# More weight-gradient jobs before the gradient's first stage, seven DMA transposes for its turn, and the prefix's stores on SyncE's queue

## The chip, the cores and the metric

The kernel runs on one core of one Trainium2 chip. The metric is the device time of one execution in microseconds (us), taken as the median over runs; lower is better. Times inside the kernel come from one profiled execution and count from the start of its span.

Names used throughout: PE is TensorE (matmuls), PEld its weight loads, DVE is VectorE, ACT is ScalarE, POOL is GpSimd and SP is SyncE. SP does no arithmetic; it issues DMAs, in the order of its queue. POOL issues DMAs too. A DMA moves data between the device memory and the on-chip memory, and one kind of it, the DMA transpose, turns blocks on the way.

## The reference

The kernel computes a forward pass of four sublayers (A, B, A, B) and its whole gradient.

```python
def _A_ref(q, k, v, shift_k, ssm_k, ssm_D):
    # k_shift: causal convolution of k with 4 taps per feature
    kv = k_shift * v
    # y: causal convolution of kv with ssm_k over 2048 positions, by FFT of length 4096
    y = y + kv * ssm_D[None, None, :]
    return q * y

def _B_ref(x, w1, w2):
    return silu(x @ w1) @ w2

x = A_q
x = x + _A_ref(_layernorm(x), A_k, A_v, A_shift_k, A_ssm_k, A_ssm_D)
x = x + _B_ref(_layernorm(x), B_w1, B_w2)
x = x + _A_ref(_layernorm(x), A_k, A_v, A_shift_k, A_ssm_k, A_ssm_D)
x = x + _B_ref(_layernorm(x), B_w1, B_w2)
```

The inputs are in bf16: 2048 positions by 448 features, `w1` 448 x 1792, `w2` 1792 x 448. Outputs are `x` and the gradients with respect to `A_q`, `A_k`, `A_v`, `shift_k`, `ssm_k`, `ssm_D`, `w1` and `w2` for a given `grad_out`. The convolution result `y` depends on neither `x` nor the layer, so it is computed once; its gradient is summed over both A layers and goes back through the transform once.

## The kernel before

The program has three parts.

**The prefix** (`_ssm_prefix`, about the first 95 us) computes `y`. The long convolution is a transform in two stages. Stage 1 is a matmul with `M1sb` for each of 16 values of `n2`. Its result is turned in seven groups of 16 blocks of 128 x 128 (`turn` on PE, or a DMA transpose from SP, L369). Stage 2 is a matmul with `Gsb` over 14 chunks of 1024 columns. It does this for the kernel `ssm_k` (tiles `A1K`, `Z`) and for `kv` (tiles `A1kv`, then `A1K`'s memory). For `kv`, `conv` makes the four-tap convolution on PE, copies it to `ks` on ACT (L385), stores it in the device memory as `KS_d` (L387, on POOL's queue) and multiplies it by `v` on DVE; `ks` has four buffers. The spectrum product needs the spectrum `Ka` and the same with its upper and lower 64 rows exchanged (`KB`): `_swap_halves_dma` (L249, L250) makes `KB` with two DMAs per piece, seven pieces, on POOL's queue. Both spectra are stored for the gradient (`SPEC_d`, L413 and L448, on POOL's queue). `cons_prod` copies a chunk of the `kv` spectrum, multiplies it on DVE into `pa` (with `Ka`, L451) and `pb` (with `KB`, L452), and the inverse stage 2 (L232, L233) follows on PE. After the prefix, in the top-level function, SP loads `w1sb` (two DMAs, L186 and L187) and `w2sb` (L189); they reuse the memory of `M1sb` and `v_n`.

**The main part** (`Main.run`, to about 515 us) handles the 2048 positions in four chunks `c` of four tiles `tl` of 128. It runs forward through the layers, then back. Matmuls with `w1`, `w2` and their transposes fill PE. The backward chunk of the first layer pair (`L == 0`) is `ga` (L537, with `w2T`), then `gn` (L736, with `w1T`): per tile 14 matmuls into `ps_n`, a copy on ACT (L738), and on DVE and ACT the backward of two layer norms (`ln_bwd`, L711 to L723, L751 to L754), whose result goes into `gYb`, the gradient of `y`.

**The suffix** (`_ssm_suffix`) takes `gYb` back through the transform and, woven in between, computes the gradients of `w1` and `w2`. These are 2 x 14 x 32 = 896 matmuls of 128 x 448, called *jobs* (`_job`, L900). Sixteen jobs share one loaded tile `dstat` of 512 KB. For `w2`, each of 14 feature tiles takes two: a DMA transpose of `AP_d` (L896) and a plain load of `A_d` (L898); its result is copied by ACT (L913) and stored (L914). `w1` takes `GP_d` and `GH_d` likewise (L960, L936, L928, L929). There are three `dstat` buffers in the pool `dp` and two more in `dp2`, which opens with the suffix.

Jobs are handed out by a generator. `fill(n)` puts `n` of them behind the last matmul in the main part: in `ga` for `c >= 1`, two behind the first group and one behind each of the others (8 in all), and in `gn` two behind each of four tiles. Only the jobs of the first two feature tiles (64) are open to `fill`; 56 are taken. In the suffix `weave(n)` puts `n` behind the last pinned matmul, and `_in_turn` pins PE's order. A load is traced when its first job is handed out; where buffers are free a planner may place it earlier on SP's queue, and instructions on every queue are ordered by that planner, except where `issue_after(i)` places an instruction behind `i` on `i`'s engine.

The suffix starts with 16 first-stage groups (`_fft_stage1`, L210): two matmuls into a PSUM buffer, of which there are two, and a copy to `A1g` (L111 on ACT for the first 12). Four jobs follow each. Then `A1g` is turned into `Zg` in seven groups. Groups 4, 5 and 6 are DMA transposes on SP (L1008); groups 0 to 3 are 16 transposes each on PE (L1014) and a copy; 16 jobs follow each group. `spectrum(cp)` then needs group `cp` of `Zg`, and loads two pieces of the stored spectra (`kk_c`, L1022 and L1023); `spectrum(0)` and `spectrum(1)` come first, then 16 jobs, then `inverse` and `spectrum` in alternation with jobs in between. At the end `grad_k(g)` computes eight pieces of the gradient of `A_k` on DVE (L1117, L1119) and stores them (L1123) on SP's queue, behind which the last job loads stand.

Of the kernel before, what the change touches and what calls it, by code (L numbers as in the profile page):

```python
# [11 lines left out]
BF16 = mybir.dt.bfloat16  # L12
# [5 lines left out]
P = 128  # L18
S = 2048
D = 448  # L20
F = 1792
J = 16
NT = 16
# [96 lines left out]
@with_exitstack  # L120
def kernel(
    ctx: ExitStack,
    tc: tile.TileContext,
    A_q: bass.AP,
    A_k: bass.AP,
    A_v: bass.AP,
    A_shift_k: bass.AP,
    A_ssm_k: bass.AP,
    A_ssm_D: bass.AP,
    B_x: bass.AP,  # L130
    B_w1: bass.AP,
    B_w2: bass.AP,
    grad_out: bass.AP,
    out_0: bass.AP,
    out_1: bass.AP,
    out_2: bass.AP,
    out_3: bass.AP,
    out_4: bass.AP,
    out_5: bass.AP,
    out_6: bass.AP,  # L140
    out_7: bass.AP,
    out_8: bass.AP,
):
    nc = tc.nc
    k = K()
    k.tc, k.nc = tc, nc
    k.bal = _Bal(nc)
    for nm, v in (("A_q", A_q), ("A_k", A_k), ("A_v", A_v), ("A_shift_k", A_shift_k), ("A_ssm_k", A_ssm_k),
                  ("A_ssm_D", A_ssm_D), ("B_w1", B_w1), ("B_w2", B_w2), ("grad_out", grad_out)):
        setattr(k, nm, v)  # L150
    k.outs = [out_0, out_1, out_2, out_3, out_4, out_5, out_6, out_7, out_8]
    C = make_fft_consts()

    dram = ctx.enter_context(tc.tile_pool(name="dram", bufs=1, space=DRAM))
    k.KS_d = dram.tile([S, D], BF16, name="KS_d")
    k.SPEC_d = {nm: dram.tile([128, SPEC], BF16, name=f"spec_{nm}") for nm in ("K", "KV")}
    k.N_d = [dram.tile([S, D], BF16, name=f"N_d{i}") for i in range(4)]
    k.DT_d = dram.tile([4, 2, P, NF // 2, 512], BF16, name="DT_d")
    k.A_d = dram.tile([P, NF, NT, P], BF16, name="A_d")
    k.AP_d = dram.tile([NF, P, S], BF16, name="AP_d")  # L160
    k.GH_d = dram.tile([P, NF, NT, P], BF16, name="GH_d")
    k.GP_d = dram.tile([NF, P, S], BF16, name="GP_d")

    bf = mybir.dt.np(BF16)
    m1b = np.ascontiguousarray(C["M1"], dtype=np.float32).astype(bf)
    minv = (np.transpose(m1b.astype(np.float32), (3, 1, 2, 0)) * np.float32(C["inv_scale"])).astype(bf)
    k.m1_h = nc.inline_tensor(np.ascontiguousarray(m1b.reshape(P, -1)), name="c_m1")
    gs_h = nc.inline_tensor(np.ascontiguousarray(C["Gs"].reshape(P, -1)).astype(np.float32).astype(bf), name="c_gs")
    k.minv_h = nc.inline_tensor(np.ascontiguousarray(minv.reshape(P, -1)), name="c_minv")

    keep = ctx.enter_context(tc.tile_pool(name="keep", bufs=1))
    k.ident = keep.tile([P, P], BF16, name="ident")
    make_identity(nc, k.ident[:])
    k.gs_h = gs_h
    k.rstd = [keep.tile([P, J], FP32, name=f"rstd{i}") for i in range(4)]
    k.warm = keep.tile([P, 4], FP32, name="warm")
    k.mhalf = keep.tile([P, 4], FP32, name="mhalf")
    nc.gpsimd.memset(k.mhalf[:], -0.5)
    nc.scalar.activation(k.warm[:], k.mhalf[:], ACT.Silu)
    k.wk = ctx.enter_context(tc.tile_pool(name="wk", bufs=1))  # L180
    k.dp = ctx.enter_context(tc.tile_pool(name="dp", bufs=1))
    k.yk = ctx.enter_context(tc.tile_pool(name="yk", bufs=1, side="right", reuse_waits="tile"))
    k.Ysb = k.yk.tile([P, J, D], BF16, name="Ysb", tag="Y")
    _ssm_prefix(k)
    k.w1sb = k.wk.tile([P, ND, F], BF16, name="w1sb", tag="WA")
    nc.sync.dma_start(out=k.w1sb[:, 0:3, :], in_=k.B_w1[0:384].rearrange("(c p) f -> p c f", p=P))  # L186
    nc.sync.dma_start(out=k.w1sb[:, 3, :], in_=k.B_w1[320:448])  # L187
    k.w2sb = k.wk.tile([P, NF, D], BF16, name="w2sb", tag="WB")
    nc.sync.dma_start(out=k.w2sb[:], in_=k.B_w2.rearrange("(c p) d -> p c d", p=P))  # L189
    k.psum = ctx.enter_context(tc.tile_pool(name="psum", bufs=1, space=PSUM, reuse_waits="tile"))  # L190
    k.xg = ctx.enter_context(tc.tile_pool(name="xg", bufs=1, side="right", reuse_waits="tile"))
    k.Xp = k.xg.tile([P, NT, 512], BF16, name="X", tag="X")
    k.X = k.Xp[:, :, :D]
    k.gYb = k.xg.tile([P, NT, D], BF16, name="gYb", tag="GY")
    k.bal.reset()
    with ExitStack() as es:
        m = Main(k, es)
        m.run()
    _ssm_suffix(k)
# [87 lines left out]
def _ssm_prefix(k):  # L287
# [4 lines left out]
    with ExitStack() as es:  # L292
# [81 lines left out]
        def conv(h, jq):  # L374
            ds = slice(h * DH, (h + 1) * DH)
            pc = psum.tile([P, 4, 256], FP32, name="ps_cv", tag="A", bufs=4)
            for u in range(4):
                j = 4 * jq + u
                for e in range(2):
                    for t in range(4):  # L380
                        js = (j - t) % J
                        src = kT[:, js // 4, 2 * h + e, js % 4, 1:129] if j >= t else kT[:, js // 4, 2 * h + e, js % 4, 0:128]
                        nc.tensor.matmul(pc[:, u, e * DC:(e + 1) * DC], lhsT=src, rhs=diag[:, 2 * h + e, t, :], start=(t == 0), stop=(t == 3))  # L383
            ks = work.tile([P, 4, DH], BF16, name="ks", tag="pa", bufs=4)
            nc.scalar.copy(ks[:], pc[:, :, :DH])  # L385
            bal.add("act", 0.95)
            nc.gpsimd.dma_start(out=_pm(k.KS_d[:])[:, 4 * jq:4 * jq + 4, ds], in_=ks[:])  # L387
            kvt = work.tile([P, 4, DH], BF16, name="kvt", tag="pb", bufs=4)
            nc.vector.tensor_tensor(out=kvt[:], in0=ks[:], in1=vn[:, 4 * jq:4 * jq + 4, ds], op=ALU.mult)
            bal.add("dve", 0.62)  # L390
            return kvt
# [14 lines left out]
        def cons_ka(ci, ps):  # L406
            sl = slice(ci * 1024, (ci + 1) * 1024)
            _copy(nc, bal.pick(1024), Ka[:, sl], ps[:])
            if ci % 2 == 1:
                lo, hi = (ci - 1) * 1024, (ci + 1) * 1024  # L410
                if ci > 8:
                    _swap_halves_dma(k, KB, Ka, lo, hi, nc.gpsimd)
                nc.gpsimd.dma_start(out=k.SPEC_d["K"][:, lo:hi], in_=Ka[:, lo:hi])  # L413

        k.na0 = k.dp.tile([P, 4, D], BF16, name="na0", tag="dstat", bufs=3)
        prev = None
# [10 lines left out]
                if h == 1:  # L427
                    _fft_stage2(k, Z, psum, cons_ka, range(2 * i, 2 * i + 2))
        for i in range(4):
            _swap_halves_dma(k, KB, Ka, 2048 * i, 2048 * (i + 1), nc.gpsimd)  # L430
        stage1_kv(*prev)
        A1f = A1kv[:].rearrange("p a c n s -> p a (c n s)")
        for i in range(3):
            _fft_stage2(k, Z, psum, cons_ka, range(8 + 2 * i, 10 + 2 * i))
            turn(A1f, Zkv, i)
        B1 = A1kv[:].rearrange("p a c n s -> p a (c n s)")
        Zf = A1K[:].rearrange("p a c n s -> p (a c n s)")

# [4 lines left out]
        def cons_prod(ci, ps):  # L443
# [1 line left out]
            xs = Zf[:, sl]  # L445
            _copy(nc, bal.pick(1024), xs, ps[:])
            if ci % 2 == 1:
                nc.gpsimd.dma_start(out=k.SPEC_d["KV"][:, (ci - 1) * 1024:(ci + 1) * 1024], in_=Zf[:, (ci - 1) * 1024:(ci + 1) * 1024])  # L448
            pa = work.tile([P, 1024], BF16, name="pa", tag="pa", bufs=4)
            pb = work.tile([P, 1024], BF16, name="pb", tag="pb", bufs=4)  # L450
            nc.vector.tensor_tensor(out=pa[:], in0=xs, in1=Ka[:, sl], op=ALU.mult)  # L451
# [28 lines left out]
class Main:  # L480
# [245 lines left out]
    def gn(self, c, L, ghT, nb, gres, na, hook=None):  # L726
# [5 lines left out]
        for tl in range(4):  # L732
# [6 lines left out]
            k.bal.add("act", 0.75)  # L739
            k.pe_engine = mm.ins.engine  # L740
            if L == 0:
                self.fill(2)
            if hook:
                hook(tl, mm.ins, last_u.ins)
            g1 = G[:, tl, :]
# [36 lines left out]
    def run(self):  # L782
# [29 lines left out]
        for c in range(4):  # L812
# [26 lines left out]
            na, nb = na1, nb1  # L839
            if c < 3:  # L840
                gb = gb_next
        k.jobs = _gw2(k, k.dp, range(2), [(k.dp, "dstat", 3)], first=k.go_jobs.ins)
        bb = nc.cur_bb.bb

        def fill(n):
# [119 lines left out]
def _ssm_suffix(k):  # L965
# [7 lines left out]
    with ExitStack() as es:  # L973
# [5 lines left out]

        def jobs():  # L980
            yield from k.jobs
            yield from _gw2(k, k.dp, range(2, NF), both)
            yield from _gw1(k, dp2, both)

        jobs = jobs()
# [9 lines left out]
        Z = sp.tile([P, NDH, P], BF16, name="Zg")  # L995
        ksf = k.yk.tile([P, J, D], BF16, name="ksf", tag="Y")
        B1k = A1[:].rearrange("p a c n s -> p (a c n s)").rearrange("p (q d) -> p q d", d=D)
        for n2 in range(16):
            with _in_turn(k):
                _fft_stage1(k, n2, k.gYb[:, n2, :], A1, psum, nc.scalar if n2 < 12 else None)  # L1000
            weave(4)
        with tc.tile_pool(name="sspec2", bufs=1, reuse_waits="tile") as p1:
            Zf = Z[:].rearrange("p a b -> p (a b)")
            A1f = A1[:].rearrange("p a c n s -> p a (c n s)")
            for g in (4, 0, 1, 2, 3, 5, 6):
                if g > 3:
                    with tc.issue_after(k.job_load):
                        nc.sync.dma_start_transpose(out=Z[:, 16 * g:16 * g + 16, :], in_=A1f[:, 16 * g:16 * g + 16, :].rearrange("p a b -> p (a b)"))  # L1008
                    weave(NT)
                    continue  # L1010
                pt = psum.tile([P, 16, P], BF16, name="ps_tr", **mm)
                with _in_turn(k):
                    for i in range(16):
                        nc.tensor.transpose(pt[:, i, :], A1f[:, 16 * g + i, :], k.ident[:])  # L1014
                weave(NT)
                _copy(nc, bal.pick(2048, dve_ns=0.53), Z[:, 16 * g:16 * g + 16, :], pt[:])

            def spectrum(cp):
                lo, hi = cp * 2048, (cp + 1) * 2048
# [88 lines left out]
        def grad_k(g):  # L1108
# [3 lines left out]
            for j in range(4):  # L1112
# [7 lines left out]
                    last = acc  # L1120
                else:
                    last = pj
            nc.sync.dma_start(out=out2_pm[:, 2 * g:2 * g + 2, :], in_=gk[:])  # L1123

        out3_pm = _pm(k.outs[3][0])
        out2_pm = _pm(k.outs[2][0])
# [89 lines left out]
```

## Time and profile before

| what | us |
|---|---|
| median of 4 runs | 750.69 |
| lowest and highest run | 749.1 and 752.15 |
| the profiled execution | 746.83 |
| its span, first to last instruction | 745.0 |
| PE busy, of the span | 690.6 (93%) |
| DVE busy | 507.1 (68%) |
| ACT busy | 424.3 (57%) |
| POOL busy | 61.6 (8%) |

The page gives each engine's busy time over the span. A busy engine need not be the one that sets the end: the page's chain of waits follows the last instruction back, at each step to what released it. By engine that chain is PE 46%, DVE 24%, DMA 9%, ACT 8%, time without a visible wait 7%, POOL 2%. The page's DMA table counts 172.77 MB, 149.46 MB of them on SP's and ACT's kind of queue and 22.19 MB on POOL's.

A line of a timeline reads: start, duration, engine, source line, operation, output<-input, shapes, count, and in brackets how long the engine was idle before and what released it. "SPq" is SP's instruction stream: a DMA's duration there is the time that SP spent issuing it, not the time to landing. Medians from issue to landing in this profile: 13.1 us for `KB<-Z`, 5.4 for `KS_d<-ks`, 4.8 for `Zg<-A1g`, 4.7 for `dstat<-A_d`, 5.3 for `dstat<-AP_d`.

### The profile page before, as it was taken

How to read it: one execution, taken by the hardware profiler on the slowest of the kernel's cores; microseconds unless marked ns; L12 is line 12 of the kernel's file. 1: busy time of each engine (PE TensorE's matmuls, PEld its weight loads, DVE VectorE, ACT ScalarE, POOL GpSimd, SP SyncE). 2: the span in 40 equal slices, each digit the busy share in tenths (PEclk: the TensorE clock that was granted, in tenths of full speed). 3: DMA queues.
4: the chain of work that ended last, by engine and by line, in shares of the span. 5: the costliest groups of instructions: out<-in, count | busy, mean ns of one | idle time of the engine just before them, and what ended most of it. 6: DMA issues, size and time to landing. Idle time of an engine off the chain costs nothing.

```text
span 745.0 us, 12143 instructions
## 1 busy us (share of the span) xinstructions
PE 690.6 (93%) x4724; PEld 363.4 (49%) x4753; DVE 507.1 (68%) x1059; ACT 424.3 (57%) x539; POOL 61.6 (8%) x109
## 2 busy tenths in 40 slices
PE   6988789999999998999999999994999999999996
PEld 5866533444344443444444443442556667555543
DVE  4878878787743596995949979886108773597241
ACT  4688767767437578487576577644525666321001
POOL 1144221111100002000000000000000000000000
PEclk9999999999999999999999999997999999999999
DMA  9979948998575878879999986965998998999786
GB/s 314 231 187 273 347 181 291 276 252 244 161 153 146 199 169 197 186 208 204 219 246 268 368 238 173 303 161 132 286 212 234 336 312 260 315 230 251 170 208 138
DMA packets 232869, 172.77 MB, mean 232 GB/s; under 512 B 178890, under 2 KB 215566, under 8 KB 231660
## 3 DMA queue, kind: packets, MB, share of 16 engines
q1 hardware_dynamic: 226446, 149.46, 76.8%
q0 software_dynamic: 5744, 22.19, 9.0%
q8 instruction: 37, 0.61, 0.3%
q10 hardware_dynamic: 622, 0.35, 0.2%
q14 instruction: 20, 0.16, 0.1%
HBM read 62.24 MB, written 63.77 MB: 169 GB/s over the span
## 4 chain that ended last, share of the span: by engine, by line
PE 46%; DVE 24%; DMA 9%; ACT 8%; issue 7%; POOL 2%; another core or an unknown queue 2%; SPq 1%; ACTq 0%; DVEq 0%; POOLq 0%
PE ps_d L900 17%; PE ps_h L537 6%; PE ps_o L654 5%; PE ps_g L537 4%; DMA KB<-Z 4%; PE ps_n L736 4%; DVE dT L113 3%; DVE lb_junk L711 3%; DVE lb_u L722 2%; PE ps_v L233 2%; PE ps_v L232 2%; DVE lb_u L754 2%; DMA K_sb<-in_A_ssm_k_dram 1%; PE ps_cv L383 1%
## 5 line engine op out<-in xcount | busy, mean ns | idle before, releaser
L900 PEld LDWEIGHTS <-dstat 128*128 128x128 bf16 x896 | 85.4, 98 | 82.1 <-issue 5.6
L537 PE MATMUL ps_h<-nT,w1sb 128*128 128x512 bf16 (+1 forms) x432 | 102.2, 386 | 7.7 <-DVE dT L113 5.1
L537 PE MATMUL ps_g<-gT,w2T 128*128 128x512 bf16 (+1 forms) x448 | 96.0, 381 | 3.3 <-ACT ghp L686 3.3
L736 PE MATMUL ps_n<-w1T,ghT 128*128 128x448 bf16 x448 | 90.2, 353 | 2.2 <-DVE ghT L694 2.0
L900 PE MATMUL ps_d<-mov,dstat 128*128 128x448 bf16 x448 | 87.7, 353 | 3.6 <-DMA dstat<-GP_d 1.8
L629 ACT ACTIVATE aT<-ps_h 128x1024 bf16<-128x1024 f32 (+1 forms) x64 | 58.4, 915 | 56.5 <-PE ps_h L537 39.5
L654 PE MATMUL ps_o<-w2sb,aT 128*128 128x448 bf16 x448 | 90.1, 353 | 0.0
L113 DVE CAST dT<-ps_h 128x1024 bf16<-128x1024 f32 (+1 forms) x55 | 58.3, 1063 | 29.1 <-ACT aT L629 29.1
L537 PEld LDWEIGHTS <-w1sb 128*128 128x128 bf16 (+1 forms) x448 | 36.1, 97 | 70.8 <-issue 42.5
L537 PEld LDWEIGHTS <-w2T 128*128 128x128 bf16 (+1 forms) x448 | 35.3, 96 | 62.2 <-issue 29.6
L736 PEld LDWEIGHTS <-ghT 128*128 128x128 bf16 x448 | 42.8, 98 | 44.2 <-DVE ghT L694 4.3
L686 ACT CAST ghp<-ps_g 128x1024 bf16<-128x1024 f32 x56 | 55.4, 1006 | 15.0 <-PE ps_g L537 11.4
L654 PEld LDWEIGHTS <-aT 128*128 128x128 bf16 x448 | 42.4, 98 | 42.3 <-issue 3.6
L900 PE MATMUL ps_d<-X,dstat 128*128 128x448 bf16 x224 | 54.5, 359 | 0.2
L900 PE MATMUL ps_d<-GO,dstat 128*128 128x448 bf16 x224 | 51.7, 353 | 0.2
L960 ACT CAST dout<-ps_d 128x448 bf16<-128x448 f32 x14 | 7.5, 534 | 67.4 <-PE ps_d L900 42.6
L738 ACT ACTIVATE lb_u<-ps_n,rstd 128x448 f32<-128x448 f32 x32 | 20.2, 633 | 40.5 <-DVE X L723 17.7
L233 PEld LDWEIGHTS <-pb 128*128 128x128 bf16 x336 | 32.9, 99 | 9.3 <-DVE pb L452 5.9
L232 PEld LDWEIGHTS <-pa 128*128 128x128 bf16 x336 | 33.3, 99 | 7.2 <-DVE pa L451 4.2
L694 DVE TENSOR_TENSOR ghT<-dT,ghp 128x1024 bf16<-128x1024 bf16 (+1 forms) x32 | 19.7, 620 | 20.4 <-ACT ghp L686 20.3
L614 ACT ACTIVATE dTl<-dTl 128x1024 bf16<-128x1024 bf16 (+1 forms) x32 | 29.8, 943 | 4.5 <-DMA dTl<-DT_d 4.5
L655 DVE TENSOR_TENSOR X<-X,ps_o 128x448 bf16<-128x448 bf16 x32 | 19.7, 615 | 16.3 <-PE ps_o L654 16.2
(187 smaller groups left out, 1091.2 us busy)
## 6 DMA issues: line engine op xcount, KB each, us to landing
DT_d<-dT SPq DMA_DIRECT2D x8, 896.0 KB, 6.3
AP_d<-aT SPq DMA_DIRECT2D x8, 896.0 KB, 4.1
A_d<-turned SPq DMA_DIRECT2D x8, 896.0 KB, 4.0
GH_d<-turned SPq DMA_DIRECT2D x8, 896.0 KB, 4.5
dTl<-DT_d SPq DMA_DIRECT2D x8, 896.0 KB, 7.4
dstat<-A_d SPq DMA_DIRECT2D x14, 512.0 KB, 4.7
GP_d<-ghT SPq DMA_DIRECT2D x8, 896.0 KB, 9.9
dstat<-GH_d SPq DMA_DIRECT2D x14, 512.0 KB, 4.3
```

The lines of the kernel that those rows point to most:

```text
L113: eng.tensor_copy(out, in_)
L232: nc.tensor.matmul(o, lhsT=pa[:, i * P:(i + 1) * P], rhs=k.Gsb[:, ga, :], start=True, stop=False)
L233: nc.tensor.matmul(o, lhsT=pb[:, i * P:(i + 1) * P], rhs=k.Gsb[:, gb, :], start=False, stop=True)
L537: self.nc.tensor.matmul(o, lhsT=w[lo:hi, b, f:f + P], rhs=r, start=(seen[u] == 1), stop=(seen[u] == ND))
L614: self.k.last_slope = self.nc.scalar.activation(s, s, ACT.Derivative_silu)
L629: last = nc.scalar.activation(a, ps[:, 0:n, :], ACT.Silu)
L654: nc.tensor.matmul(po[:, :D], lhsT=aT[ft // 7][0][:, ft % 7, tl * P:(tl + 1) * P], rhs=self.w2sb[:, ft, :], start=(ft == 0), stop=(ft == N ...
L686: k.last_gh = nc.scalar.copy(gh[:], ps[:])
L711: nc.vector.scalar_tensor_tensor(out=junk[:], in0=u0, scalar=1.0, in1=n_t, op0=ALU.mult, op1=ALU.mult, accum_out=cp[:, 1:2])
L736: mm = nc.tensor.matmul(pn[:, :D], lhsT=ghT[ft // 7][:, ft % 7, tl * P:(tl + 1) * P], rhs=self.w1T[:, ft, :], start=(ft == 0), stop=(ft == ...
L738: last_u = nc.scalar.activation(u0[:], pn[:, :D], ACT.Identity, scale=k.rstd[2 * L + 1][:, t:t + 1], accum_out=cp[:, tl, 0:1])
L900: i = k.nc.tensor.matmul(ps[:, :D], lhsT=st[:, t, :], rhs=mov[:, t, :], start=start and t == 0, stop=stop and t == NT - 1)
```

## The change

There are four edits. The loads of `w1sb` and `w2sb` move from the top-level function into the prefix, behind the loop over the last three pieces of `ssm_k`'s spectrum; and the stores of `KS_d` and `SPEC_d` and the half swaps are issued by SP in place of POOL. The generator open to `fill` gets the jobs of three feature tiles (96) in place of two, and `gn` of the last chunk fills 12 in place of 2 behind each tile. The suffix weaves 16 jobs ahead of the first stage, all seven groups of `Zg` are DMA transposes in the order 0 to 6, and 8 jobs in place of 16 follow each. The last two stores of `grad_k` (`g` 6 and 7) are issued by POOL.

```diff
@@ top-level function @@
     _ssm_prefix(k)
-    k.w1sb = k.wk.tile([P, ND, F], BF16, name="w1sb", tag="WA")
-    nc.sync.dma_start(out=k.w1sb[:, 0:3, :], in_=k.B_w1[0:384].rearrange("(c p) f -> p c f", p=P))
-    nc.sync.dma_start(out=k.w1sb[:, 3, :], in_=k.B_w1[320:448])
-    k.w2sb = k.wk.tile([P, NF, D], BF16, name="w2sb", tag="WB")
-    nc.sync.dma_start(out=k.w2sb[:], in_=k.B_w2.rearrange("(c p) d -> p c d", p=P))
@@ _ssm_prefix @@
-            nc.gpsimd.dma_start(out=_pm(k.KS_d[:])[:, 4 * jq:4 * jq + 4, ds], in_=ks[:])
+            nc.sync.dma_start(out=_pm(k.KS_d[:])[:, 4 * jq:4 * jq + 4, ds], in_=ks[:])
...
-                    _swap_halves_dma(k, KB, Ka, lo, hi, nc.gpsimd)
-                nc.gpsimd.dma_start(out=k.SPEC_d["K"][:, lo:hi], in_=Ka[:, lo:hi])
+                    _swap_halves_dma(k, KB, Ka, lo, hi, nc.sync)
+                nc.sync.dma_start(out=k.SPEC_d["K"][:, lo:hi], in_=Ka[:, lo:hi])
...
         for i in range(4):
-            _swap_halves_dma(k, KB, Ka, 2048 * i, 2048 * (i + 1), nc.gpsimd)
+            _swap_halves_dma(k, KB, Ka, 2048 * i, 2048 * (i + 1), nc.sync)
         stage1_kv(*prev)
...
             turn(A1f, Zkv, i)
+        k.w1sb = k.wk.tile([P, ND, F], BF16, name="w1sb", tag="WA")
+        nc.sync.dma_start(out=k.w1sb[:, 0:3, :], in_=k.B_w1[0:384].rearrange("(c p) f -> p c f", p=P))
+        nc.sync.dma_start(out=k.w1sb[:, 3, :], in_=k.B_w1[320:448])
+        k.w2sb = k.wk.tile([P, NF, D], BF16, name="w2sb", tag="WB")
+        nc.sync.dma_start(out=k.w2sb[:], in_=k.B_w2.rearrange("(c p) d -> p c d", p=P))
...
-                nc.gpsimd.dma_start(out=k.SPEC_d["KV"][:, (ci - 1) * 1024:(ci + 1) * 1024], in_=Zf[:, (ci - 1) * 1024:(ci + 1) * 1024])
+                nc.sync.dma_start(out=k.SPEC_d["KV"][:, (ci - 1) * 1024:(ci + 1) * 1024], in_=Zf[:, (ci - 1) * 1024:(ci + 1) * 1024])
@@ Main.gn @@
-                self.fill(2)
+                self.fill(2 if c < 3 else 12)
@@ Main.run @@
-        k.jobs = _gw2(k, k.dp, range(2), [(k.dp, "dstat", 3)], first=k.go_jobs.ins)
+        k.jobs = _gw2(k, k.dp, range(3), [(k.dp, "dstat", 3)], first=k.go_jobs.ins)
@@ _ssm_suffix @@
-            yield from _gw2(k, k.dp, range(2, NF), both)
+            yield from _gw2(k, k.dp, range(3, NF), both)
...
+        weave(NT)
         for n2 in range(16):
...
-            for g in (4, 0, 1, 2, 3, 5, 6):
-                if g > 3:
-                    with tc.issue_after(k.job_load):
-                        nc.sync.dma_start_transpose(out=Z[:, 16 * g:16 * g + 16, :], in_=A1f[:, 16 * g:16 * g + 16, :].rearrange("p a b -> p (a b)"))
-                    weave(NT)
-                    continue
-                pt = psum.tile([P, 16, P], BF16, name="ps_tr", **mm)
-                with _in_turn(k):
-                    for i in range(16):
-                        nc.tensor.transpose(pt[:, i, :], A1f[:, 16 * g + i, :], k.ident[:])
-                weave(NT)
-                _copy(nc, bal.pick(2048, dve_ns=0.53), Z[:, 16 * g:16 * g + 16, :], pt[:])
+            for g in range(7):
+                with tc.issue_after(k.job_load):
+                    nc.sync.dma_start_transpose(out=Z[:, 16 * g:16 * g + 16, :], in_=A1f[:, 16 * g:16 * g + 16, :].rearrange("p a b -> p (a b)"))
+                weave(NT // 2)
...
-            nc.sync.dma_start(out=out2_pm[:, 2 * g:2 * g + 2, :], in_=gk[:])
+            (nc.sync if g < 6 else nc.gpsimd).dma_start(out=out2_pm[:, 2 * g:2 * g + 2, :], in_=gk[:])
```

`NT` is 16. `_swap_halves_dma` issues two DMAs of 256 KB on the queue that it is given.

## The prediction

> **What bounds the kernel now.** I read the page's busy times first, then stretches, then the chain of waits and the timelines of the four places that the diff touches. TensorE is busy 690.6 of 745.0 us, so only its gaps, and work taken off it, can pay. The stretches show where they are (columns: PE, weight loads, DVE, ACT, POOL busy, granted clock, DMA share, GB/s):
>
> ```profile
> 60.00:85.00 25.00, 21.30 (x268) 15.55 (x269) 21.20 (x28) 23.53 (x24) 6.65 (x13) 1.00 1.04 294
> 505.00:515.00 10.00, 1.50 (x8) 0.69 (x7) 9.16 (x28) 2.86 (x6) 0.00 (x0) 0.76 0.51 126
> 515.00:520.00 5.00, 3.59 (x10) 1.43 (x10) 0.39 (x1) 3.48 (x5) 0.54 (x1) 0.50 0.24 93
> 535.00:560.00 25.00, 24.95 (x177) 14.63 (x177) 2.81 (x3) 5.67 (x6) 0.00 (x0) 1.00 1.02 207
> ```
>
> One large hole at 505 to 516, after it a clock of 0.50; at 535 to 560 PE is full and the DMA engines are too. The timeline of the hole:
>
> ```profile
> 505.58 0.92 PE L900 MATMUL ps_d<-GO,dstat 128*128 128x448 bf16 x4
> 514.81 0.76 ACT L716 ACTIVATE lb_v<-na_l,lb_cc 128x448 bf16<-128x448 bf16 x1 [4.26 <-DVE lb_cc L713]
> 515.48 1.69 ACT L111 CAST A1g<-ps_s 128x896 bf16<-128x896 f32 x2
> 516.41 0.90 PE L210 MATMUL ps_s<-gYb,M1s 128*128 128x448 bf16 x2 [9.91 <-ACT A1g L111]
> ```
>
> PE has nothing to do because the third L210 needs a PSUM buffer, its copy stands on ACT behind lb_v, and lb_v waits for DVE's backward normalization of the last chunk. The prefix, in the chain of waits, hangs on half swaps:
>
> ```profile
> 58.29 12.11 DMA KB<-Z
> 70.68 14.48 DMA KB<-Z
> ```
>
> SyncE's (SP's) queue after the gradient's first stage, and at the end of the kernel, where the store of gk (L1123) waits for DVE and the next jobs' loads stand behind it:
>
> ```profile
> 534.85 1.97 SPq L1008 DMA_TRANSPOSE Zg<-A1g  x1
> ...
> 539.90 3.16 SPq L1008 DMA_TRANSPOSE Zg<-A1g  x1
> ...
> 543.74 3.83 SPq L1008 DMA_TRANSPOSE Zg<-A1g  x1
> ```
> ```profile
> 720.60 1.24 SPq L936 DMA_TRANSPOSE do<-dout  x1
> 723.48 0.34 SPq L1123 DMA_DIRECT2D out_dram<-gk  x1
> 723.92 3.15 SPq L896 DMA_TRANSPOSE dstat<-GP_d  x1
> ```
>
> **The change, part by part.** A job is one L900 matmul: 34 of them took 6.43 us in the chain, 0.189 each.
>
> *Part B, more jobs at the last chunk's end.* 4 x 10 extra jobs between the four ps_n groups and 16 ahead of the first stage are 56 jobs, 10.6 us of PE work. Now the last ps_n group would start at 491.96 + 3 x (26 x 0.189) = 506.7, the fills end at 491.96 + 104 x 0.189 = 511.6, the 16 at 514.6, two L210 groups with four jobs each at 516.9; ACT's copy, moved from 515.48 by at most the 0.8 us that the ps_n groups lag DVE's 4.74 us per tile, is there by 517.2. So the 9.91 us are filled, and with no pause the slow restart goes: 12 matmuls from 516.41 to 520.44 took 4.03 us where 12 x 0.189 is 2.27, 1.8 lost. B = -11.7. Loads: the jobs need A_d of the third tile (issued at 492.15) only at 506, and two more loads whose buffers come free at 500 and 506, wanted at 511.6 and 514.6, against 4.5 to 5.2 us to land. Bounds: 0 if those loads come late, -11.7.
>
> *Part C, seven DMA transposes.* PE loses 64 transposes: 0.89 us per 16 in the chain (537.44, 541.36), -3.6. Four PSUM copies (1.23 and 1.86 us) leave DVE and ACT, which have room. SP gets four more transposes, and all seven now stand in one run: those loads after which they are ordered were issued before the first stage ended, and the next job loads, written later, wait for buffers that come free only after it. By part B the stage ends near 532.8 (514.6 and 16 groups of 1.14, the chain's 521.92 to 523.06) with 176 jobs done (now 120 at 533.65); turns start at 534.0. PE then has 56 jobs (10.6), two spectra (8 x 0.22 + 8 x 0.189 = 3.2), 16 jobs (3.0) and a first inverse (0.9): at 550.6 it wants the load behind the turns, which lands at 534.0 + 7p + 5.2 (median of L896). The stall is 7p - 11.4. For p, one turn's time on SP, the nearest rows are the three above, mean 2.99: 20.9 us, a stall of 9.5. C = -3.6 + 9.5 = +5.9. Bounds for p: 1.97 (stall 2.4) and 5.03, the longest of the prefix's three L369 turns.
>
> [...]
>
> *Part D, the last two gk stores on GpSimd's (POOL's) queue.* SP's wait to 723.47 makes the load at 723.92 late by 1.8 (the round before: 720.60 - 714.25 = 6.35, 715.91 + 6.35 = 722.3), and the second wait, to 728.72, makes the one at 729.18 late; PE waited 1.28 for the first and 1.21 for the second. D = -2.5. POOL then waits for gk; behind it stand the dout memsets, next due at 734.36, later than gk's 728.72: nothing. Bounds 0 and -3.
>
> *Part A, the prefix on SP's queue.* 36 issues (8 KS_d, 14 swaps, 14 spectrum stores) of 0.5 to 0.8 us leave POOL, 61.6 us busy in all, which the chain shows for 2%. Gain: the 3.36 MB of w1 and w2, issued from 54.01, went ahead of the swaps; at the 294 GB/s of the first row above they are 11.4 us. Swaps first would land the last at about 74 instead of 85.2, and DVE's waits for KB (0.69, 2.52, 0.19) go: -3.4. The weights land at 73.5 to 85.0 now and are wanted at 103.6: hidden, and worth what the backlog outlasts 103 if not. Loss: the KS_d stores now stand behind three transposes that hold SP from 26.04 to 36.8. The fifth ks copy (ACT, 38.53) reuses the first one's buffer; with the median 5.4 us to landing it is free at 42.2, 3.7 late, on an ACT that is busy 4.56 of 5 us there, so on the path: behind it on ACT are na and the A1kv copies, and PE waits for those. A = +0.3. Bounds: -3.4 (the stores go in between) and +5.1 (the longest landing, 10.2). SP's wait for KV data holds up only the x0c loads, issued at 90.61 after the last of those stores (89.72 on POOL).
>
> [...]
>
> Sum: -11.7 + 5.9 - 2.5 + 0.3 = -8.0. The profiled execution took 746.83 (span 745.0 and 1.83 around it), 3.86 under the median 750.69. 746.83 - 8.0 = 738.8, at the median's level **742.7**. The forecast's own range is p from 1.97 (-15.1, 735.6) to the prefix's mean of 3.53 with the slow restart (-2.4, 748.3).
>
> **Rivals.** (1) *Turns hidden.* The job loads slip in between the turns, or a turn takes 2 us; no stall: -17.5, 733.2, and 729.5 with the prefix's best. For it: two turns of ghT, 896 KB, took 3.86 us of SP. Against: DMA share 1.02 from 535 to 560. (2) *Order undone.* The weights still go out ahead of the swaps (w2's load was issued ahead of w1's, though written after it, so written order isn't kept): A = +3.7. And a job load stands behind the spectrum loads (L1022), which waited for the store of G to 519.14 and were through at 521.5: it lands at 526.0 where PE wants it at 523.7, +2.3; with the restart's 1.8 the sum is -8.0 + 3.4 + 2.3 + 1.8 = -0.5, 750.2. (3) *Starved by the turns: slower.* A turn takes 4.13, the prefix's median, and the load for the 16 jobs between the first two spectra and the inverse also falls behind the seven. PE wants it at 546.7 and gets it at 534.0 + 28.9 + 4.5: 20.7 us, 22.5 with the restart; -17.5 + 22.5 + (0 to 0.3) gives +5.0, 755.7. It decides from 7p = 23.9, a turn of 3.4 us. For it: SP had hardly a pause from 535 to 561. Against: a part of those times was job loads.
>
> **How the numbers follow.** Forecast 0.45, turns hidden 0.22, order undone 0.13, starved 0.20. What a measurement here can tell is 0.3%, 2.25 us. Faster takes the forecast but for its end and rival 1; same takes rival 2; slower takes rival 3: 0.69, 0.13, 0.18. The range runs from rival 1's best, 729, to rival 3, 756, which leaves out what lies beyond either.
>
> **What would show it.** B: no PE gap over 1 us from 492 to 534, the clock at 1.00 there. C: seven Zg turns in one run on SP, then a wait of PE for dstat near 550; its length gives p. D: no PE wait for dstat after 700. A: no DVE wait for KB, an ACT pause near 38. I am wrong if PE starves already before the first stage, if the turns are spread, or if the prefix moves by more than 4 us.

## The result, and the profile after

The changed kernel took 751.56 us (median of 39 runs), the kernel before 747.97 beside it (64 runs, up to 753.05): a ratio of 1.0047, 95% interval 1.0031 to 1.0062. It is slower by 0.5% (3.6 us), where 8.0 us faster was forecast (742.7, against the 750.69 of the kernel before at that time). Ratios are of undisturbed runs alone, so a ratio need not be that of two medians. The profiled execution took 750.37 us, span 748.6 (before 745.0).

Its stretches, in the columns of those shown of before:

```profile
60.00:85.00 25.00, 22.26 (x284) 16.63 (x287) 22.43 (x29) 22.97 (x25) 0.00 (x0) 1.00 1.02 311
505.00:515.00 10.00, 10.00 (x55) 5.16 (x54) 9.42 (x29) 3.39 (x7) 0.00 (x0) 1.00 0.79 184
515.00:520.00 5.00, 4.06 (x22) 2.03 (x21) 3.12 (x10) 2.11 (x3) 0.54 (x1) 1.00 0.84 240
535.00:560.00 25.00, 18.59 (x106) 9.57 (x105) 10.34 (x18) 4.54 (x6) 0.00 (x0) 0.97 1.14 226
560.00:580.00 20.00, 15.32 (x136) 10.53 (x138) 8.47 (x15) 8.79 (x10) 0.00 (x0) 0.78 0.92 274
```

The hole at 505 is gone and the clock there is 1.00. A new one stands at 535 to 580: PE idles 6.4 us, then 4.7 more with a clock of 0.78. PE's timeline gives both places:

```profile
519.49 0.54 PE L205 MATMUL ps_s<-gYb,M1s 128*128 128x448 bf16 x2 [0.94 <-ACT A1g L111]
...
564.63 2.04 PE L900 MATMUL ps_d<-X,dstat 128*128 128x448 bf16 x5 [9.92 <-DMA dstat<-AP_d]
```

9.91 us of waiting for ACT became 0.94, and 9.92 us of waiting for a load came instead. SP's timeline has that load behind the seven turns:

```profile
532.09 5.84 SPq L896 DMA_TRANSPOSE dstat<-AP_d  x1
538.02 0.53 SPq L898 DMA_DIRECT2D dstat<-A_d  x1
538.65 9.48 SPq L1008 DMA_TRANSPOSE Zg<-A1g  x3
548.24 0.53 SPq L914 DMA_DIRECT2D out_dram<-dout  x1
548.81 10.01 SPq L1008 DMA_TRANSPOSE Zg<-A1g  x4
...
559.81 2.60 SPq L896 DMA_TRANSPOSE dstat<-AP_d  x1
```

The run is 538.65 to 558.8, 20.2 us, 2.88 a turn. The list of PE's waits over the whole span (total, times, longest):

```profile
PE ps_d L900 <- DMA dstat<-AP_d: 12.0, 2, 9.9
...
PE ps_cv L378 <- DVE Z L113: 3.7, 1, 3.7
...
PE ps_d L900 <- DMA dstat<-GP_d: 3.3, 3, 1.7
```

The second wait for `AP_d`, 2.1 us, ends at 592.75: the buffers, once empty, were not full again (from 569.3 to 578.0 SP stood at a spectrum load, L1015, that waits for DVE). The prefix's wait was 2.2 before, and the waits at the end 1.8 for `GP_d` and 1.2 for `GH_d`.

### The profile page after: what moved, and what is told of

The parts are those of the page before. It is cut to its first block, busy times and chain, and to the rows that moved or that the text cites. A ratio compares the mean times of both kernels' runs of the same rounds, so it can differ in the third digit from the quotient of the medians.

```text
span 748.6 us, 12009 instructions
## 1 busy us (share of the span) xinstructions
PE 687.8 (92%) x4660; PEld 360.5 (48%) x4689; DVE 505.1 (67%) x1057; ACT 420.6 (56%) x537; POOL 41.8 (6%) x75
## 5 line engine op out<-in xcount | busy, mean ns | idle before, releaser
L537 PE MATMUL ps_h<-nT,w1sb 128*128 128x512 bf16 (+1 forms) x432 | 100.7, 381 | 7.7 <-DVE dT L113 5.2
L614 ACT ACTIVATE dTl<-dTl 128x1024 bf16<-128x1024 bf16 (+1 forms) x32 | 29.8, 943 | 6.8 <-DMA dTl<-DT_d 6.8
L1047 DVE TENSOR_TENSOR pa<-Zg,kk_c 128x1024 bf16<-128x1024 bf16 x28 | 19.3, 690 | 18.2 <-PE ps_v L227 18.0
```

What stands on the lines that cost most here:

```text
L537: self.nc.tensor.matmul(o, lhsT=w[lo:hi, b, f:f + P], rhs=r, start=(seen[u] == 1), stop=(seen[u] == ND))
L614: self.k.last_slope = self.nc.scalar.activation(s, s, ACT.Derivative_silu)
```

## The experiments

My theory after the result: the run of turns starves the jobs, and the other parts do what they were said to. The first four kernels have one part of the change each.

**e1, part A alone.**

```diff
-_swap_halves_dma(k, KB, Ka, lo, hi, nc.gpsimd)
+_swap_halves_dma(k, KB, Ka, lo, hi, nc.sync)
...
(the prefix's stores on nc.sync, the weight loads behind the spectrum loop)
```

> The kernel before with the prefix edit alone (stores, swaps and weight loads on SP's queue). Theory (the prefix's gain and loss cancel): within 1.5 us of before, ratio 0.998 to 1.002; the wait of PE for the fifth ks copy grows from 2.2 to about 3.7 us, and DVE's 2.5 us wait for KB is gone. Rival (the prefix is where the loss comes from): 3 to 5 us slower, ratio 1.004 to 1.007.

Measured: 1.0005 [0.9984, 1.0026]. A is worth nothing in sum.

**e2, part B alone.**

```diff
-                self.fill(2)
+                self.fill(2 if c < 3 else 12)
...
+        weave(NT)
```

> The kernel before with 12 jobs behind each tile of the last chunk and 16 ahead of the first stage, and with the turns as before (four groups on PE, three by DMA). Theory (the hole before the first stage is real PE time, and only the seven turns gave it back): 9 to 12 us faster, ratio 0.984 to 0.988, no PE wait over 1 us for dstat. Rival (the part after the first stage is bound by DMA, so time won before it is lost there whatever turns Zg): ratio 0.996 to 1.002, with a PE wait for dstat of 5 us or more between 540 and 600.

Measured: 0.9937 [0.9908, 0.9966], about 4.7 us faster, half of what the theory gave. (Its profile is of a run of 746.39, the longest of the twelve, whose median is 743.93.) The hole is filled as in the changed kernel. What is given back stands in PE's waits from 605 on, where the kernel before has 3.0 us of such waits:

```profile
PE ps_d L900 <- DMA dstat<-GP_d: 7.5, 5, 3.6
```

Two of them, of 3.61 and 2.30 us, are followed by slow jobs, which cost another 1.6 and 1.5. SP's timeline shows a load that stands behind a waiting store:

```profile
635.27 0.53 SPq L1098 DMA_DIRECT2D out_dram<-gK  x1
644.47 0.40 SPq L928 DMA_DIRECT2D out_dram<-do  x1
...
645.54 2.38 SPq L896 DMA_TRANSPOSE dstat<-GP_d  x1
```

The store of a turned tile `do` goes out 8.7 us after the instruction ahead of it, when the turn has landed, and the next load of `GP_d` comes only then. SP's waits for such turns from 600 on, in the kernel before and in e2 (total, times, longest):

```profile
SPq L928 <- DMA do<-dout: 5.9, 7, 1.8
```
```profile
SPq L928 <- DMA do<-dout: 16.6, 6, 6.1
```

The 56 jobs done early bring the `w1` jobs forward: the first load of `GP_d` is at 602.39, in before at 620.33. But the last one is at 729.14, in before at 730.93, so the lead of 17.9 us has shrunk to 1.8. From 664 to 690 SP has no pause and takes 7.8 to 9.8 us from one load of `GP_d` to the next; before has such gaps there too (8.2 to 10.5) and no wait, so the gaps alone don't make PE wait.

**e3, part C alone.**

```diff
-            for g in (4, 0, 1, 2, 3, 5, 6):
+            for g in range(7):
...
+                weave(NT // 2)
```

> The kernel before with all seven groups of Zg turned by DMA and 8 jobs behind each, and without the extra jobs. Theory (seven turns in one run on SP hold up the next job load): a run of about 20 us on SP, a PE wait for dstat of 8 to 12 us near 550 to 560, slow restart; with 3.6 us less PE work 6 to 11 us slower, ratio 1.008 to 1.015. Rival (the turns cost nothing by themselves and only the 56 jobs moved ahead run the buffers dry): 3 to 4 us faster, ratio 0.995 to 0.996.

Measured: 1.0120 [1.0089, 1.0151], 9.0 us slower. PE's and SP's timelines:

```profile
558.37 3.07 PE L900 MATMUL ps_d<-X,dstat 128*128 128x448 bf16 x8 [8.26 <-DMA dstat<-AP_d]
```
```profile
551.78 1.33 SPq L1007 DMA_TRANSPOSE Zg<-A1g  x1
553.21 2.76 SPq L896 DMA_TRANSPOSE dstat<-AP_d  x1
```

The same wait, at the same place, without parts A, B and D, as the theory had it.

**e4, part D alone.**

```diff
-nc.sync.dma_start(out=out2_pm[:, 2 * g:2 * g + 2, :], in_=gk[:])
+(nc.sync if g < 6 else nc.gpsimd).dma_start(out=out2_pm[:, 2 * g:2 * g + 2, :], in_=gk[:])
```

> The kernel before with the last two stores of gk on POOL's queue alone. Theory now (other loads on SP keep the same spacing in the tail, as in the changed kernel): 0 to 1 us faster, ratio 0.999 to 1.000. Rival (the prediction's step): the waits of 1.28 and 1.21 us for dstat go, 2.5 us faster, ratio 0.9965 to 0.9975.

Measured: 0.9985 [0.9959, 1.0010]; no change shown. The four parts add up to 1.0047, the change's own ratio; each has an interval of 0.2 to 0.3% to either side, so that the sum is known to some 0.5%.

**e5, the change without part C.** The changed kernel with `for g in (4, 0, 1, 2, 3, 5, 6)` and its body as before.

> The changed kernel with its one part C undone: parts A, B and D are there, and Zg is turned as before (four groups by PE, three by DMA). My theory says that the run of seven turns is the whole loss: with e2 (more jobs only) at 0.9937 of before, A at 1.0005 and D between 0.996 and 1.001, this one should stand at 0.990 to 0.995 of before (740 to 744 where before has 747.5), with no wait on PE over 2 us between 535 and 605 us. Rival: the four parts disturb each other whatever turns Zg (A and D load the queues, B's jobs use up the buffers); then the loss stays, 1.000 to 1.005 of before, and PE still waits for dstat<-AP_d after the first stage.

Measured: 0.9948 [0.9927, 0.9968], and no wait over 2 us between 535 and 605. C is the loss, 7.4 us on top of the rest (1.0047 less 0.9948). At the end this kernel waits as e2 does: 6.3 us for `GP_d`, and SP 16.7 us for the turns of `do`.

**e6, the turns spread.** Groups 2 to 6 of `Zg` read `A1` when the inverse has already written its first chunks there, so their values differ.

```diff
+                if g < 2:
+                    turn_g(g)
...
+                if cp + 2 < NCI // 2:
+                    turn_g(cp + 2)
                 inverse(cp, prev)
```

> The changed kernel with the same seven DMA turns, but only groups 0 and 1 are issued ahead of the first spectrum; groups 2 to 6 are each issued one spectrum ahead of their use, so that loads of jobs lie between them on SP. The bytes moved and the number of turns are the same. My theory says that the 9.92 us wait came from seven turns in a row on SP with a load of a job behind them, not from what the turns move: the wait for dstat<-AP_d falls under 3 us, the slow restart goes too, and the time is 0.990 to 0.996 of before (740 to 745). Rival: the stretch 535 to 560 us is bound by what the 16 DMA engines can move (the page shows them full there, 1.14 of their share), so the loads come late however the turns are ordered; then PE still waits 8 us or more in sum for AP_d between 535 and 605 us and the time stays at 1.002 to 1.006.

Measured: 1.0017 [0.9990, 1.0044]. PE waits for `AP_d` no more, but the longest of its waits from 537 to 605 is a new one, and ACT's list says for what:

```profile
PE ps_v L227 <- ACT A1g L111: 7.0, 1, 7.0
```
```profile
ACT A1g L111 <- DMA Zg<-A1g: 10.0, 2, 7.6
```

The inverse's copies go into `A1`, which a late turn still reads. The named wait went as the theory said, the time did not; the experiment does not tell order from volume.

**e7, e2 with the stores of `gk` and `ksf` on POOL; e8, those of the turned `do` tiles too.**

```diff
-            nc.sync.dma_start(out=out3_pm[:, sl, :], in_=ksf[:, sl, :])
+            nc.gpsimd.dma_start(out=out3_pm[:, sl, :], in_=ksf[:, sl, :])
...
-            nc.sync.dma_start(out=out7w[:, :, ft * P:(ft + 1) * P], in_=o7[:, 0:3, :])
+            nc.gpsimd.dma_start(out=out7w[:, :, ft * P:(ft + 1) * P], in_=o7[:, 0:3, :])
```

> Part B alone, and all stores of gk and of ksf in the suffix (sixteen) issued by POOL instead of SP. In e2 (B alone) PE waits 4.3 us for dstat<-GP_d between 655 and 690 us, where the trace of before shows none: B's jobs bring the w1 jobs forward, so that their loads, turns and stores meet the stores of gk and ksf on SP. If that crowding of SP's queue is where e2's missing 4 to 5 us went, this one has less than 1 us of such waits before 690 us and stands 3 to 5 us under e2, 0.987 to 0.990 of before (738 to 740). Rival: the loads are late by the DMA engines' own share (1.01 between 605 and 690 us in e2); then a store moved to another queue changes nothing, the waits stay at 3 to 5 us and the ratio at 0.992 to 0.996.

> As e7, and the stores of the turned do tiles of the w1 jobs (two for each of twelve tiles) issued by POOL as well. In e2 SP stands 8.9 us, 6.1 at the longest, at such a store that waits for its turn to land, with loads of jobs behind it. If SP's standing there is what makes the loads late, this one loses the waits for GP_d that e7 leaves after 690 us (3.3 us in e2) as well: 0.983 to 0.988 of before (735 to 738.5). Rival: the loads wait for a free buffer and not for SP, then it equals e7 within 0.2%; or POOL's memset of dout, now behind these stores, holds up ACT's copies and it is slower than e7 by 1 to 3 us.

Measured: e7 0.9886 [0.9860, 0.9912], e8 0.9789 [0.9765, 0.9813]. e7's time is the theory's, but its waits for `GP_d` before 690 are 3.4 us, not under 1; e8 is faster than the theory had it and has no such wait in the suffix at all. The stretch 605 to 690 of e2 and of e8:

```profile
605.00:690.00 85.00, 80.68 (x642) 49.11 (x641) 56.49 (x86) 33.12 (x39) 3.67 (x8) 0.99 1.01 257
```
```profile
605.00:690.00 85.00, 84.95 (x816) 51.77 (x816) 56.26 (x82) 30.65 (x36) 20.72 (x39) 1.00 1.09 290
```

With more moved (290 against 257 GB/s, DMA share 1.09 against 1.01) PE is full: not the DMA engines but SP's order had made the loads late. SP has no wait for a turn of `do` any more, and the lead holds: the first load of `GP_d` is at 597.94 and the last at 708.21, each over 22 us earlier than in the kernel before. e8, at 731.13 us, is 2.1% under the kernel before and 2.6% under the changed one. What the moved stores are worth without part B, no run tells.

**e9, the turns issued by ACT; e10, the same on e8.**

```diff
-                    nc.sync.dma_start_transpose(out=Z[:, 16 * g:16 * g + 16, :], ...)
+                    nc.scalar.dma_start_transpose(out=Z[:, 16 * g:16 * g + 16, :], ...)
...
+        if 4 <= ft <= 8:
+            nc.vector.tensor_copy(o[:], ps[:, :D])
```

> The changed kernel with its seven turns issued by ACT instead of SP, at the same places of the program; five copies of dout (w2 tiles 4 to 8) go from ACT to DVE, so that they don't stand behind the turns. The turns, their bytes and their place in time are the same; what changes is that no load of a job stands behind them on SP. My theory says that SP's order was the cause: the loads of AP_d are issued among the turns, the wait for dstat<-AP_d falls from 12.0 us in sum to under 4, and the time to 0.992 to 0.998 of before (741.5 to 746). Rival: the engines that move the data were the limit (seven turns and two loads of AP_d, nine pieces of 512 KB at 2.9 us each, are 26 us, against 19 us of jobs ready to run): the turns slow to 4 us or more each with loads beside them, PE waits 8 us or more in sum for AP_d or for the turned groups, and the time stays at 1.001 to 1.006.

> The kernel of e8 (more jobs, all stores of the suffix on POOL) with the seven turns on ACT as in e9. The turns take 64 transposes off PE, 3.6 us by the rows of before. If they hide when no load stands behind them, this one is 2 to 4 us under e8's 731.1 (0.974 to 0.977 of before); if the rival of e9 holds, the starved stretch costs what it does there and this one is 3 to 9 us over e8 (735 to 740, 0.983 to 0.990).

Measured: e9 1.0170 [1.0120, 1.0221], e10 1.0131 [1.0105, 1.0158], slower than either side said. The chain of waits of e9:

```profile
543.53 4.90 DMA Zg<-A1g
548.47 0.04 issue
548.51 4.46 DMA dstat<-AP_d
552.99 3.02 ACTq L1011
...
560.80 4.59 DMA Zg<-A1g
565.43 0.04 issue
565.48 4.24 DMA dstat<-AP_d
569.74 2.02 ACTq L1011
```

Twice here a load of `AP_d`, a transpose on SP, started when a turn on ACT had landed (548.51 after 548.43, 565.48 after 565.39), and ACT's next turn when that load had (552.99 after 552.97, 569.74 after 569.72). The seven turns hold ACT for 30.7 us (541.05 to 571.76), and ACT's copies of `Zg` stand behind them: PE waits 24.2 us for these, and for no load of `AP_d`. What made the two queues wait for each other, no run here shows.

**e11, the change with e8's stores on POOL.** The changed kernel with the diff of e7 and e8.

> The changed kernel, all four parts as they are with the turns on SP, and the stores of gk, ksf and the turned do tiles on POOL as in e8. It stands to e8 as the changed kernel stands to e5, by part C (A is worth nothing by e1). The changed kernel's waits for dstat<-GP_d in the suffix are 3.3 us, e5's 6.3 and e2's 7.5. My theory says that the price of C belongs to the stretch 537 to 605 us and is independent of the end: PE idles 12 to 14 us there as in the changed kernel, the suffix's waits go, and the time is 4 to 8 us under the changed kernel's (0.994 to 0.999 of before), 12 to 16 us over e8. Rival: part of C's price is an exchange with the end (jobs that PE could not run early are run late, when it would have waited anyway); then, with the end's waits gone, C costs 8 us or less over e8, and the time is 0.986 to 0.990 of before.

Measured: 1.0022 [1.0003, 1.0041], 17 us over e8, 2 under the changed kernel and not 4 to 8. From 537 to 605 PE idles 12.5 us (e8: 0.5), and the waits for `GP_d` are gone. So C costs more, not less, where the end is free. Of the 17, 12 are that idle time and 3.2 stand at 380 to 500, which the point on A takes up.

**e12 and e13, six and four turns ahead of the load.** e12 is e8 with part C and `weave(NT)` after each turn; e13 is e8 with five groups by DMA.

```diff
-            for g in (4, 0, 1, 2, 3, 5, 6):
-                if g > 3:
+            for g in (2, 0, 3, 1, 4, 5, 6):
+                if g > 1:
```

> The kernel of e8 with all seven turns on SP, and sixteen jobs after each turn instead of eight. The order on SP is then six turns, a load of AP_d, the seventh turn, where the changed kernel has seven turns and then the load. My theory: PE's wait for that load is the number of turns ahead of it by 2.88 us, less 11.4 us that the jobs with data cover: 5.9 us here (9.92 and 9.3 us were measured behind seven), and the time is e8's 731.1, less 3.6 for PE's transposes, plus 5.9 and 1.7 for the restart: 735 (733 to 738, 0.981 to 0.987 of before). Rival: what counts is how much is moved (seven turns and the loads of the stretch), not what stands ahead of what; then PE waits 9 us or more in sum for AP_d, as in the changed kernel, and the time is 739 or more (0.988 and up).

> The kernel of e8 with five groups turned by DMA and two by PE; the order on SP is four turns, a load of AP_d, the fifth turn. My theory: 4 by 2.88 less 11.4 is 0.1 us, so PE waits under 1 us for AP_d, and two groups less on PE are worth 2 by 0.9 us: 729.3 (728 to 731, 0.974 to 0.978 of before). Rival, bound by what is moved: the wait grows with the number of turns whatever their place, from three turns (no wait) to seven (9 to 10 us), so 4 us or more here, and the time is 733 or more.

Measured: e12 0.9968 [0.9945, 0.9990], e13 0.9874 [0.9836, 0.9912]; both slower than e8. PE's and SP's timelines, e12 and then e13:

```profile
560.39 4.51 PE L900 MATMUL ps_d<-X,dstat 128*128 128x448 bf16 x16 [10.50 <-DMA dstat<-AP_d]
565.84 3.20 PE L900 MATMUL ps_d<-GO,dstat 128*128 128x448 bf16 x16 [0.94 <-DMA dstat<-A_d]
```
```profile
553.34 1.82 SPq L1008 DMA_TRANSPOSE Zg<-A1g  x1
555.26 2.24 SPq L896 DMA_TRANSPOSE dstat<-AP_d  x1
```
```profile
553.29 4.83 PE L900 MATMUL ps_d<-X,dstat 128*128 128x448 bf16 x16 [3.02 <-DMA dstat<-AP_d]
```
```profile
543.85 4.52 SPq L1009 DMA_TRANSPOSE Zg<-A1g  x2
548.46 2.29 SPq L896 DMA_TRANSPOSE dstat<-AP_d  x1
```

The waits, 10.5 and 3.0 us, are neither of my 5.9 and 0.1; by its bounds e12 speaks for the rival; e13's wait lies between both, and its time (736.42) is in the rival's range. Taken apart, each wait has two ends:

| kernel | turns ahead | first turn | load issued | per turn | jobs run out | load lands |
|---|---|---|---|---|---|---|
| changed | 7 | 538.65 | 559.81 | 3.02 | 554.7 | 564.6 |
| e3 | 7 | 535.02 | 553.21 | 2.60 | 550.1 | 558.4 |
| e12 | 6 | 537.77 | 555.26 | 2.92 | 549.9 | 560.4 |
| e13 | 4 | 536.91 | 548.46 | 2.89 | 550.3 | 553.3 |

"Per turn" is from the first turn to the load's issue, with the stores in between, by the number of turns; "jobs run out" is PE's start after the wait less the wait. The load goes out right behind the turns ahead of it, however many follow, and lands 4.8 to 5.2 us later: its landing goes by the order, as the theory has it. What I had wrong is the cover: 16.1 us from the first turn on in the changed kernel, but 12.1 and 13.4 here, because sixteen jobs after each turn use up the loaded buffers and leave no spectrum or inverse among them. Why a turn takes 2.9 us, SP's issuing or the DMA engines (share 1.02 to 1.14 there), no run tells.

## Why the prediction was wrong

**Part B, -11.7: the step that failed most.** Its working held at its place: 0.94 us of wait left, a clock of 1.00, the first stage through at 534.79 with 176 jobs done. But alone it measured -4.7 (e2), 7.0 short. The step took for granted that 56 jobs less at the end shorten the end by as much. In e2's profile PE waits 7.5 us for loads there, where the kernel before waits 3.0, and two slow restarts cost 3.1: 7.6 us more. The loads stood on SP's queue behind stores that wait; with 40 stores off that queue (e8) the waits are gone and the time is 11 us below e2's (0.9937 less 0.9789, of 747). The bound 0 was named for another reason, loads late at 506 to 515, which were not.

**Part C, +5.9: right in cause and stall, too small in sum.** A turn was put at 2.99 us and took 2.88 (182 GB/s for its 512 KB); the stall at 9.5, measured 9.92. That the stall came out so well is in part luck: the first turn went out at 538.65 and not at 534.0, behind a load that held SP to 537.93, and the jobs ran out at 554.7 and not at 550.6, and these two cancel. Alone C measured +9.0 (e3's interval is 6.6 to 11.3), on top of the rest 7.4 (e5). The forecast priced the stall but not what follows it: the slow restart, which it had priced at 1.8 for the hole of part B and which is some 2.1 here (five jobs in 2.04 us, then the first inverse's matmuls 0.107 us apart where they are 0.055 apart otherwise); the wait of 2.1 at 592 on buffers not yet refilled, with a restart of some 1.5 of its own; and 0.8 for a copy of `Zg`. With these and the measured stall, 5.9 becomes 12.8. In return the end waits less: 3.3 us for `GP_d`, where e5 has 6.3 and two restarts of 3.1 together. The balance is 6.7, near the 7.4. Where e8's stores have freed the end (e11) there is nothing to get back, and C costs more.

**Part D, -2.5: not shown.** e4 shows -1.1 [-3.1, +0.8], which leaves room for it, but the waits that were to go are there: 2.6 us for `GP_d` at the end in e4 and 3.3 in the changed kernel, where before has 1.8 and 1.2 for `GH_d`. Two stores were a small part of what stands in that queue; e7 and e8 moved sixteen and forty.

**Part A, +0.3: right in sum, by other terms.** The gain came as forecast: the first weights go out behind the swaps, at 74.63, and DVE's waits for `KB` are gone. The loss did not: the fifth `ks` copy waits 0.64 us in the changed kernel, as before (1.28 in e1), and not 3.7; the three transposes held SP to 34.25 and not to 36.8. PE's wait for the prefix's convolution grew all the same, from 2.2 to 3.7, now for DVE's copy of `Z`. And a loss that the forecast has not stands in the main part: PE's longest wait for `ghp` is 2.5 to 4.0 us in every profile with part A and 1.1 to 1.5 in those without; in the changed kernel it is at 403, where ACT's L614 waits for a load of `dTl` (6.8 us in sum from 380 to 500, before 4.5). How the prefix's queue reaches a load 300 us later stays open.

**The sum.** 0.4 - 4.7 + 9.0 - 1.1 = +3.6, the measured difference. Rival 3 named the right side (+5.0), but not by its mechanism: a turn took 2.88 us and not 4.13, less than the 3.4 that it needed, and the load for the 16 jobs was not behind the turns. The sign was decided by B's missing 7 and C's extra 3.

## What to carry to other kernels

Work moved out of a late stage pays only if that stage can go faster (here 4.7 of the 11.7 us priced): before taking the gain, look on the queue that issues its loads for stores that wait ahead of them (here 16.6 us against 5.9). Price a stall with what follows it, the slow restart and the emptied buffers (here 2.1 and 3.6 us after a stall of 9.92), and with the later waits that it relieves. The load behind the transposes on one queue went out only after their full time (seven of 2.88 us), so count the turns ahead of that load and the work that covers them; taking stores off the queue that loads paid more (11 us) than any reordering of the turns.

## What the runs showed of the hardware

Long pauses of PE were followed by slow matmuls, and what that cost did not grow with the pause: sixteen jobs took 4.83 us after 3.02 and 4.51 after 10.50, but 3.20 after 0.94 (e12, e13), a loss of 1.3 to 1.6 us; after 9.92 in the changed kernel it was some 2.1. There the granted clock was 0.50 from 564.6 to 567.0, and 0.52 from 592.7 to 596.0, behind the wait of 2.06. In the suffix every pause from 3.61 us up was followed so (26 jobs took 6.69 us after 3.61 in e2), and none up to 1.9 us (26 jobs took 5.09 after 1.88 in e7). Between them it went either way: 2.30 us in e2 was followed by slow jobs (1.5 us lost), 2.35 in e7 was not, nor was 3.2 in the main part of e11, where the granted clock was 1.00 from 380 to 500. What decides it there, no run shows.
